# Moving the first Wk chunk to second place on its DMA ring and finishing the first four key tiles one after another

## The chip, the cores and the metric

The kernel runs on one core of a Trainium2 chip. The metric is the device time of one execution in microseconds; the figure for a kernel is the median of several executions. A separate execution is profiled; its trace gives the start and the duration of every instruction, the time at which every DMA landed, and the inferred releaser of every wait. All durations in the text come from that one execution.

## What is computed

Two branches are mixed by a gate. Branch A is a linear attention over `x` (2048 rows of 512) with 32 heads of 16; branch B is a token-mixing MLP over the layer-normed `x`. Cut to what matters:

```python
phi = lambda t: jnp.where(t > 0, t + 1, jnp.exp(t)) + 1e-6
q, k, v = split(x @ wqkv)                   # per head
pq, pk = phi(q), phi(k)
kv = einsum("bhsd,bhse->bhde", pk, v);  z = einsum("bhsd->bhd", pk)
o  = (pq @ kv) / (pq @ z)
a  = o @ wo
u  = gelu(einsum("bsd,sf->bdf", layernorm(x), w1) + b1)
b  = transpose(einsum("bdf,fs->bds", u, w2) + b2)
g  = sigmoid((x * gate_w).sum(-1))
out = g * a + (1 - g) * b
```

The value projection is not formed. Since `kv` is linear in `v = x Wv`, the kernel accumulates G, the product of `x` transposed with `pk`, over all rows and multiplies the small result by `Wv` afterwards.

## The kernel before, in words

The 2048 rows are 16 tiles of 128 (index t); the 512 features are four blocks of 128 (index k). The order of instructions is written out by hand: each engine carries out its own instructions in program order, and semaphores are placed between engines where data demand it. There are five stages:

1. **Start.** All loads are queued up. Eight of 128 KB come first, four on the ring of SyncE (SP) and four on that of ScalarE (ACT), issued by `load_x` (L124) and `load_wk` (L127): x tiles 0 to 3, then the four row blocks ("chunks") of Wk. Behind them SP issues the transposing loads of `xT` for tiles 4 and later (L130) and the rest of x. For the first four tiles `xT` is made on TensorE by `transpose_tile` (L193): four 128x128 transposes into a PSUM bank, then one copy out, on VectorE (L199) for tiles 0 and 2, on ScalarE (L197) for 1 and 3. Six matmuls on constants (`warm_up`, L108) run while the first load is under way, a seventh of 256 columns between the transposes of tiles 1 and 2.
2. **Keys.** `k_part(t, ks)` adds the named chunks to the key accumulator of tile t, one 128x512 matmul per chunk. `k_phi` turns the finished accumulator into `pk`: exp on ScalarE (L203), a min-add (L204) and a max-add (L207) on VectorE. For the first four tiles (`HEADS`) the chunks go outermost: chunk 0 for tiles 0 to 3, chunk 1 for tiles 0 to 3, chunk 2 likewise, and chunk 3 last; then the four `k_phi`. From tile 4 on a loop makes per tile four key matmuls, `k_phi`, the four G matmuls of tile t - 4 (`g_tile`), and on VectorE the layer-norm statistics of tile t - 3 (`ln_step`, L227 and L228). After the loop come `g_tile` of tiles 12 to 15.
3. **First part of the MLP with the queries.** Three accumulators of `u` and one query block per step.
4. **The rest of `u`,** with the small products of branch A between.
5. **Output.** Per row tile four matmuls of branch A and fourteen of branch B, then one combination on VectorE and a store.

All matmuls are recorded at L108, so the trace tells them apart by the accumulator: `wps` warm-up, `kacc` keys, `gacc` G, `qacc` queries, `uacc` MLP, `aps` and `yps` output; `pt` holds the transposes. Accumulators come from one pool of eight PSUM banks: one that is freed is given to the next that asks, and that one must wait until the former's last reader is done. G holds four of the eight through stage 2, so `kacc` of tile t takes the bank that tile t - 4 leaves.

Of the kernel before, what the change touches and what calls it, by code (L numbers as in the profile page):

```python
# [15 lines left out]
def kernel(  # L16
# [13 lines left out]
    nc = tc.nc  # L30
# [10 lines left out]
    ND = D // P  # L41
# [25 lines left out]
    def bank(name, dtype=FP32):  # L67
        return ps.tile([P, SC], dtype, name=name, tag="bank")
# [38 lines left out]
    def mm(o, lhsT, rhs, start, stop, **kw):  # L107
        nc.tensor.matmul(o, lhsT=lhsT, rhs=rhs, start=start, stop=stop, **kw)  # L108
# [14 lines left out]
    def load_x(q, t0, n):  # L123
        q.dma_start(out=xs[:, t0 : t0 + n, :], in_=x_view[:, t0 : t0 + n, :])  # L124

    def load_wk(q, k):
        q.dma_start(out=wk_sb[:, k, :], in_=wqkv_view[:, k, D : 2 * D])  # L127

    def load_xT(t0, n):
        nc.sync.dma_start(  # L130
            out=xT[:, :, t0 * P : (t0 + n) * P], in_=X[t0 * P : (t0 + n) * P, :], transpose=True
        )

    for i in range(2):
        load_x(nc.sync, 2 * i, 1)
        load_x(nc.scalar, 2 * i + 1, 1)
    for i in range(2):
        load_wk(nc.sync, 2 * i)
        load_wk(nc.scalar, 2 * i + 1)
    load_xT(4, 2)  # L140
    load_xT(6, 2)
    load_x(nc.sync, 4, 4)
# [39 lines left out]
    def warm_up(n, cols=SC):  # L182
        for _ in range(n):
            mm(wps[:, :cols], warm[:, 0:P], warm[:, :cols], True, True)
# [5 lines left out]
    def transpose_tile(t, on_act):  # L190
        pt = bank("pt", BF16)
        for k in range(ND):
            nc.tensor.transpose(pt[:, k * P : (k + 1) * P], xs[:, t, k * P : (k + 1) * P], ident[:])  # L193
        dst = xT[:, :, t * P : (t + 1) * P]
        src = pt[:].rearrange("p (k s) -> p k s", k=ND)
        if on_act:
            nc.scalar.activation(out=dst, in_=src, func=ACT.Copy)  # L197
        else:
            nc.vector.tensor_copy(out=dst, in_=src)  # L199
# [13 lines left out]
    def k_part(t, ks):  # L213
        if t not in kaccs:
            kaccs[t] = bank("kacc")
        for k in ks:
            mm(
                kaccs[t][:], xT[:, k, t * P : (t + 1) * P], wk_sb[:, k, :],
                k == 0, k == ND - 1,
            )  # L220

    def k_phi(t):
        phi(pk[:, t, :], kaccs.pop(t))

    def ln_stats(t):
        stats = work.tile([P, nc.vector.BN_STATS_DIM], FP32, name="stats", tag="stats", bufs=2)
        nc.vector.bn_stats(out=stats[:], in_=xs[:, t, :])  # L227
        nc.vector.bn_aggr(out=mv[:, t, :], in_=stats[:])  # L228

    def ln_rstd(g):  # L230
        s = slice(g * TPC, (g + 1) * TPC)
        nc.vector.tensor_scalar_add(out=veps[:, s], in0=mv[:, s, 1], scalar1=EPS)
        nc.gpsimd.tensor_tensor(out=rstd[:, s], in0=veps[:, s], in1=mhalf[:], op=ALU.pow)
# [36 lines left out]
    def ln_step(u):  # L270
        ln_stats(u)
        if u % TPC == TPC - 1:
            ln_rstd(u // TPC)

    HEADS = 4
    transpose_tile(0, False)
    transpose_tile(1, True)
    warm_up(1, 256)
    transpose_tile(2, False)
    transpose_tile(3, True)  # L280
    ln_step(0)
    ln_step(1)
    for k in range(ND - 1):
        for t in range(HEADS):
            k_part(t, (k,))
    for t in range(HEADS):
        k_part(t, (ND - 1,))
    for t in range(HEADS):
        k_phi(t)
    LAG = 4  # L290
    LN_LAG = 3
# [218 lines left out]
```

## Time and profile before

| what | value |
|---|---|
| median of 8 runs | 166.93 us (166.57 to 167.23) |
| the profiled execution | 166.53 us |
| its span, first to last instruction | 164.6 us |
| TensorE busy (PE) | 159.1 us, 97% of the span |
| VectorE busy (DVE) | 87.6 us, 53% |
| ScalarE busy (ACT) | 58.5 us, 36% |
| first key matmul starts | 5.56 us |

PE is TensorE's matmul side, PEld its weight loads, DVE VectorE, ACT ScalarE; a q after an engine's name is its sequencer, which issues DMAs. Times of instructions count from the start of the span. Matmuls overlap in their pipeline: a 128x512 matmul lasts 379 ns in the list of groups, but the next one starts 0.216 us after it, so the distance of starts is what a matmul costs.

### The profile page before, as it was taken

To read this page: it belongs to the slowest core of one execution; us is meant where nothing else is said; L and a number is where in the kernel's file an instruction comes from. 1 tells how busy PE (TensorE), PEld (TensorE's weight loads), DVE (VectorE), ACT (ScalarE), POOL (GpSimd) and SP (SyncE) were. 2 spreads that over 40 slices of the span, in tenths; PEclk is the share of its full clock that TensorE was granted. 3 is DMA by queue.
4 is the path that set the end of the run, shared out by engine and by line. 5 is a ranking of instruction groups with operands and counts; after the bars stand their busy time and mean duration, and the time that the engine had idled before them with its cause. 6 is when DMAs were issued, how large, how long until landed. Compare 5 with 4: busy or idle time off the path is not lost.

```text
span 164.6 us, 2059 instructions
## 1 busy us (share of the span) xinstructions
PE 159.1 (97%) x772; PEld 74.0 (45%) x786; DVE 87.6 (53%) x200; ACT 58.5 (36%) x90; POOL 18.3 (11%) x37
## 2 busy tenths in 40 slices
PE   7899999999999999999999999999999999999992
PEld 2534444444544444434444444444444444444471
DVE  0579999967999999109995301156221111111131
ACT  3364284848568374221332113111122221111110
POOL 5000702200110000001055500050000000000000
PEclk9999999999999999999999999999999999999999
DMA  5999999999900005800794499932010001101001
GB/s 147 243 249 235 295 354 334 349 347 349 303 25 0 0 0 154 292 4 0 258 307 115 158 298 310 327 120 88 32 36 32 32 32 46 49 33 36 32 32 32
DMA packets 29993, 25.05 MB, mean 152 GB/s; under 512 B 7776, under 2 KB 29408, under 8 KB 29984
## 3 DMA queue, kind: packets, MB, share of 16 engines
q1 hardware_dynamic: 27968, 22.02, 44.8%
q0 software_dynamic: 1440, 2.38, 5.1%
q10 hardware_dynamic: 576, 0.52, 1.0%
q8 instruction: 6, 0.10, 0.3%
q14 instruction: 3, 0.02, 0.0%
HBM read 21.11 MB, written 2.23 MB: 142 GB/s over the span
## 4 chain that ended last, share of the span: by engine, by line
PE 93%; DMA 2%; DVE 1%; issue 1%; SPq 0%; ACT 0%
PE yps L108 29%; PE uacc L108 29%; PE gacc L108 9%; PE qacc L108 8%; PE aps L108 8%; PE kacc L108 8%; DMA wk_sb<-in_A_wqkv_dram 2%; PE denps L108 1%; PE kvps L108 1%; PE wps L108 1%; SPq L124 0%; DVE pk L207 0%; ACT e L203 0%; DVE ot L473 0%; DVE e L204 0%
## 5 line engine op out<-in xcount | busy, mean ns | idle before, releaser
L108 PE MATMUL uacc<-hs,w1c 128*128 128x512 bf16 x218 | 51.6, 379 | 0.3
L108 PE MATMUL yps<-uT,w2c 128*128 128x512 bf16 (+1 forms) x235 | 50.8, 366 | 0.2
L473 DVE SCALAR_TENSOR_TENSOR ot<-yps,c,a_sc 128x512 bf16<-128x512 f32 (+1 forms) x17 | 12.2, 720 | 46.1 <-PE yps L108 46.1
L108 PEld LDWEIGHTS <-w2c 128*128 128x128 bf16 x238 | 23.3, 98 | 25.3
L108 PEld LDWEIGHTS <-w1c 128*128 128x128 bf16 x224 | 21.7, 98 | 26.0 <-issue 0.4
L458 ACT ACTIVATE a_sc<-aps,c,gg 128x512 f32<-128x512 f32 x16 | 12.5, 778 | 46.7 <-PE aps L108 43.0
L318 ACT ACTIVATE uT<-uacc,bcol 128x512 bf16<-128x512 f32 x14 | 9.3, 687 | 27.7 <-PE uacc L108 27.7
L108 PE MATMUL qacc<-xT,wq_sb 128*128 128x512 bf16 x64 | 16.4, 379 | 0.0
L108 PE MATMUL aps<-W2sb,pqT 128*128 128x512 bf16 x62 | 16.2, 379 | 0.1
L108 PE MATMUL kacc<-wk_sb,xT 128*128 128x512 bf16 x63 | 15.7, 379 | 0.5 <-DMA wk_sb<-in_A_wqkv_dram 0.4
L108 PE MATMUL gacc<-pk,xs 128*128 128x512 bf16 x62 | 15.7, 379 | 0.3 <-DVE pk L207 0.2
L243 ACT ACTIVATE hs<-xs,nmr,rstd 128x512 bf16<-128x512 bf16 x16 | 12.8, 804 | 3.1 <-DVE nmr L237 3.1
L203 ACT ACTIVATE e<-qacc 128x512 bf16<-128x512 f32 x16 | 9.6, 597 | 10.1 <-PE qacc L108 9.2
L203 ACT ACTIVATE e<-kacc 128x512 bf16<-128x512 f32 x16 | 9.0, 595 | 8.9 <-PE kacc L108 8.9
L414 POOL DMA_DIRECT2D rex<-rd_dram x16 | 9.5, 606 | 23.0 <-DVE pqT L416 18.1
L207 DVE SCALAR_TENSOR_TENSOR pk<-kacc,e 128x512 bf16<-128x512 f32 x16 | 11.1, 692 | 0.6
L207 DVE SCALAR_TENSOR_TENSOR pqT<-qacc,e 128x512 bf16<-128x512 f32 x16 | 11.1, 692 | 0.6
L204 DVE TENSOR_SCALAR e<-e 128x512 bf16<-128x512 bf16 x32 | 9.0, 282 | 4.3 <-ACT e L203 4.3
L227 DVE BATCH_NORM_STATS2 stats<-xs 128x6 f32<-128x512 bf16 x16 | 10.9, 682 | 0.0
L108 PEld LDWEIGHTS <-xs 128*128 128x128 bf16 x64 | 6.3, 98 | 8.1 <-issue 0.8
L401 DVE CUSTOM_DVE_ANT_0 junk<-xs,gw_b 128x512 bf16<-128x512 bf16 x16 | 9.8, 680 | 0.0
L108 PEld LDWEIGHTS <-xT 128*128 128x128 bf16 x64 | 6.2, 98 | 7.9 <-ACT xT L197 0.5
(64 smaller groups left out, 73.1 us busy)
## 6 DMA issues: line engine op xcount, KB each, us to landing
w2c<-in_B_w_dram SPq DMA_DIRECT2D x4, 1792.0 KB, 8.9
w1c<-in_B_w_dram SPq DMA_DIRECT2D x2, 2048.0 KB, 15.9
w1c<-in_B_w_dram SPq DMA_DIRECT2D x3, 1024.0 KB, 11.6
rex<-rd_dram POOLq DMA_DIRECT2D x16, 128.0 KB, 3.1
out_dram<-ot SPq DMA_DIRECT2D x15, 128.0 KB, 1.7
xs<-in_A_x_dram SPq DMA_DIRECT2D x3, 512.0 KB, 4.6
wq_sb<-in_A_wqkv_dram SPq DMA_DIRECT2D x1, 512.0 KB, 6.3
wv_sb<-in_A_wqkv_dram SPq DMA_DIRECT2D x1, 512.0 KB, 11.3
```

What stands on the lines that cost most here:

```text
L108: nc.tensor.matmul(o, lhsT=lhsT, rhs=rhs, start=start, stop=stop, **kw)
L203: nc.scalar.activation(out=e[:], in_=acc[:], func=ACT.Exp)
L204: nc.vector.tensor_scalar(out=e[:], in0=e[:], scalar1=1.0, scalar2=PHI_EPS, op0=ALU.min, op1=ALU.add)
L207: nc.vector.scalar_tensor_tensor(out=dst, in0=acc[:], scalar=0.0, in1=e[:], op0=ALU.max, op1=ALU.add)
L227: nc.vector.bn_stats(out=stats[:], in_=xs[:, t, :])
L243: nc.scalar.activation(out=hs[:, t, :], in_=xs[:, t, :], func=ACT.Identity, scale=rstd[:, t : t + 1], bias=nmr[:, t : t + 1],)
L318: nc.scalar.activation(out=uT[:, j, :], in_=acc[:], func=ACT.Gelu_apprx_tanh, bias=bcol[:, j : j + 1])
L401: nc.vector.tensor_tensor_reduce(out=junk[:], in0=xs[:, t, :], in1=gw_b[:], scale=1.0, scalar=0.0, op0=ALU.mult, op1=ALU.add, accum_out=gp ...
L414: nc.gpsimd.dma_start(out=rex[:], in_=src.unsqueeze(1).to_broadcast([8, HEAD, SC]))
L458: nc.scalar.activation(out=a_sc[:], in_=aps[:], func=ACT.Identity, scale=gg[:, t : t + 1], bias=c2[:, t : t + 1],)
L473: nc.vector.scalar_tensor_tensor(out=ot[:, :W], in0=yps[:, :W], scalar=c1[:, t : t + 1], in1=a_sc[:, cs], op0=ALU.mult, op1=ALU.add,)
```

## The change

The order of the eight first loads becomes x0, Wk0, x3, Wk2 on SP and x1, x2, Wk1, Wk3 on ACT (before: x0, x2, Wk0, Wk2 and x1, x3, Wk1, Wk3). The seventh warm-up matmul is left out. After the transposes of tiles 0 to 2 come the key matmuls of chunks 0 and 1 for these three tiles, then the transposes of tile 3. Then each tile in turn gets what it lacks (chunks 2 and 3; tile 3 all four) and its `k_phi` at once. The statistics of tile 1 are written after the transposes of tile 3; nothing else of VectorE's stands between.

```diff
-    for i in range(2):
-        load_x(nc.sync, 2 * i, 1)
-        load_x(nc.scalar, 2 * i + 1, 1)
-    for i in range(2):
-        load_wk(nc.sync, 2 * i)
-        load_wk(nc.scalar, 2 * i + 1)
+    load_x(nc.sync, 0, 1)
+    load_x(nc.scalar, 1, 1)
+    load_wk(nc.sync, 0)
+    load_x(nc.scalar, 2, 1)
+    load_x(nc.sync, 3, 1)
+    for k, q in ((1, nc.scalar), (2, nc.sync), (3, nc.scalar)):
+        load_wk(q, k)
...
     transpose_tile(1, True)
-    warm_up(1, 256)
     transpose_tile(2, False)
-    transpose_tile(3, True)
     ln_step(0)
+    for k in range(2):
+        for t in range(HEADS - 1):
+            k_part(t, (k,))
+    transpose_tile(HEADS - 1, True)
     ln_step(1)
-    for k in range(ND - 1):
-        for t in range(HEADS):
-            k_part(t, (k,))
     for t in range(HEADS):
-        k_part(t, (ND - 1,))
-    for t in range(HEADS):
+        k_part(t, range(2 if t < HEADS - 1 else 0, ND))
         k_phi(t)
```

## The prediction

> **What bounds the kernel now.** I read the page first (busy shares, chain that ended last), then TensorE's own waits, then the chain of waits and the timeline of the first 20 us, then the DMA view in narrow windows, last the end of the key stage.
>
> ```profile
> PE 159.1 (97%) x772; PEld 74.0 (45%) x786; DVE 87.6 (53%) x200; ACT 58.5 (36%) x90; POOL 18.3 (11%) x37
> PE 93%; DMA 2%; DVE 1%; issue 1%; SPq 0%; ACT 0%
> ```
>
> TensorE carries 93% of the chain, so anything that shortens or lengthens its stream shows up one to one. Its waits after the first instruction are these:
>
> ```profile
> PE kacc L108 <- DMA wk_sb<-in_A_wqkv_dram: 0.4, 1, 0.4
> PE gacc L108 <- DVE pk L207: 0.2, 1, 0.2
> ```
>
> Both lie in the stage that the change touches. The chain of waits there:
>
> ```profile
> 1.73 3.79 DMA wk_sb<-in_A_wqkv_dram
> 5.52 0.04 issue
> 5.56 2.98 PE kacc L108 x13
> 8.54 0.02 issue
> 8.56 0.61 ACT e L203
> 9.17 0.02 issue
> 9.19 0.31 DVE e L204
> 9.50 0.02 issue
> 9.52 0.70 DVE pk L207
> 10.22 0.04 issue
> 10.26 1.02 PE gacc L108 x4
> ```
>
> The path runs over the landing of chunk 0 (5.52), thirteen key matmuls until tile 0 is complete, its exp and two VectorE steps (2.07 us from the start of the thirteenth matmul, 8.15, to 10.21), then the first G matmul at 10.26. TensorE fills part of that time: the last of its 20 key matmuls (16 for tiles 0 to 3, 4 for tile 4) starts at 9.66. By the spacing of 0.216 us (0.86 us per four matmuls in the chain of the loop) the next could start at 9.87, and it starts at 10.26: **0.39 us lost**, of which the waits view sees 0.2 since it counts from modelled ends. Two smaller ones of this kind: tile 5's first key matmul starts 0.28 us after its forerunner (11.19), 0.05 us after VectorE has ended pk of tile 1 (11.14), whose PSUM bank it takes: **0.06 us**. And tile 15's first G matmul, in the timeline:
>
> ```profile
> 32.18 0.69 DVE L207 SCALAR_TENSOR_TENSOR pk<-kacc,e 128x512 bf16<-128x512 f32 x1
> 32.93 0.10 PEld L108 LDWEIGHTS <-xs 128*128 128x128 bf16 x1 [0.28 <-issue]
> ```
>
> It starts 0.05 us after pk of tile 15 ends (32.87), 0.38 us after the matmul before it (32.55): **0.16 us**. After that I find no stall above 0.2 us until the end of the span.
>
> **The loads.** Issue starts and times to landing from the DMA view in windows:
>
> ```profile
> xs<-in_A_x_dram SPq DMA_DIRECT2D x1, 128.0 KB, 2.9
> ...
> wk_sb<-in_A_wqkv_dram ACTq DMA_DIRECT2D x1, 128.0 KB, 4.0
> ...
> wk_sb<-in_A_wqkv_dram ACTq DMA_DIRECT2D x1, 128.0 KB, 4.5
> ```
>
> Together with the issue times (0.81, 1.25, 1.73, 2.2 on each ring) the four places of SP's ring land at 3.60, 4.19, 5.52, 6.25 and those of ACT's at 3.78, 4.38, 5.69, 6.72. All eight are of one size, so I keep a place's landing when what it carries is changed. A rule speaks against that: the Trainium skill's page "DMA: Bandwidth & Descriptors" (Queues, rings and completion order) says that completion isn't first-in, first-out per issuing engine. By the trace each ring's four landings are in order and 0.5 to 1.3 us apart, so I take the places. The bad end: Wk0 gains nothing from its place and lands at 5.52 still. Then the path worked out below begins with three matmuls at 5.56, 5.78 and 5.99 in place of 4.77 to 5.48, the next step starts at 6.21 in place of 5.73, and 0.48 us of the sum are lost (rival 2). The good end, a landing before 4.19, gives nothing more, since the copy of tile 0 ends at 4.72.
>
> **The change part by part.**
>
> *Loads.* Wk0 comes to 4.19 (from 5.52), x2 to 4.38 on ACT (from 4.19), x3 to 5.52 (from 4.38); Wk1, Wk2 and Wk3 keep 5.69, 6.25 and 6.72. Number and order of issue behind them stay. SP's first transposing load waits 1.2 us for an x load (waits of SP's queue; it starts 0.2 us after x0 lands, as the ninth DMA) and x0 is still first; the later ones meet x1 and Wk0, landed by then. So xT of tile 4 lands at 7.92 as before.
>
> *The seventh warm-up goes.* It holds 0.11 us (4.41 to 4.52), but tile 2's transposes need x2 at 4.38 anyway: they start near 4.42 and end near 4.81, VectorE's copy (0.42) near 5.27. Worth 0.1 us there, nothing at the end, since Wk1 comes later. "TensorE: Matmul & The Clock Gate" (Parts 1 and 4) warns that the array runs at half rate until about 3.4 us of activity, and that transposes don't count as activity. The row says that the switch is past: transposes are 0.107 us apart up to 4.26 and 0.056 from 4.36, before the removed matmul starts, and TensorE's idle gap that follows, 0.42 us, becomes shorter. By the rule read strictly it would cost as worked out under rival 3; by the row nothing. I take the row.
>
> *Chunks 0 and 1 of tiles 0 to 2.* Tile 0's copy ends at 4.72, tile 1's at 5.21, tile 2's near 5.27: the three chunk-0 matmuls start at 4.77, 5.26, 5.48. Chunk 1 lands at 5.69: 5.73, 5.95, 6.16. These six have all started by the time at which before only three had.
>
> *Tile 3's transposes* now wait in TensorE's stream for x3 (5.52) ahead of everything else; at 6.38 it is there. Four of 0.056 us: to 6.60. They only change places, so they cost nothing in sum. If x3 came later than 6.38, all that follows would shift one to one. ScalarE's copy runs 6.80 to 7.40 (it was 5.17 to 5.77), ahead of exp of tile 0.
>
> *Finish in turn.* Tile 0 chunk 2 starts at 6.60 (landed 6.25), chunk 3 at 6.82 (landed 6.72, ready 6.76). Nine matmuls remain from there, 1.94 us, so tile 4's first starts at 8.76; before it was 9.01. **Gain 0.25 us.** Tile 3's own start at 7.90, its copy done at 7.40; xT of tile 4 (7.92) is in time by 0.8 us.
>
> *pk of tile 0.* Complete at 7.20, exp from 7.36 (ScalarE's copy delays it by 0.12), pk done at 7.36 + 1.65 = 9.01. G of tile 0 can start at 8.76 + 4 x 0.216 = 9.62: no wait. **Gain 0.39.** pk of tile 1 follows by 0.93 (VectorE's distance in the timeline): 9.94, and tile 5 asks for that bank at 10.49: **gain 0.06.** The number of bank requests and the order of their release stay, so the bank is that of tile 1 still; this is inferred, not seen.
>
> *pk of tile 15.* VectorE is without an idle stretch from 9.19 to 32.87 in the timeline, so its start sets its end: 1.2 us earlier, 31.67. TensorE, 0.70 us earlier, asks at 32.07. **Gain 0.16.** ScalarE's exp stays 0.3 us or more ahead of VectorE.
>
> Sum: 0.25 + 0.39 + 0.06 + 0.16 = **0.86 us**. What is late next: nothing by 0.4 us; the landings after stage 2 lie far ahead of use (first W1 chunk 28.8 of some 33.6; xT of tile 12 at 17.4). The tail after the last matmul is unchanged. Profiled execution: 166.53 - 0.86 = 165.67, span 163.8. That execution is 0.40 under the median of the eight runs, and I take the same gain from the median: **166.05 us**.
>
> **Rivals.**
>
> 1. *Part of the gain.* Either Wk1 or Wk3 lands up to 0.4 us later than its place says, or tile 5 gets tile 2's bank (pk 10.86, so a start at 10.91 instead of 10.49). For: landings differ by 0.2 to 0.5 us between the two rings at one place. Against: bytes ahead are equal. Gain about 0.45: 166.5.
> 2. *It doesn't do what it says:* Wk0 lands no sooner than 5.52. Tile 3's transposes then stand in TensorE's stream after the first key matmuls instead of before, and tile 4 starts 0.22 us later than now; yet pk of tile 0 is still ready before G asks, so three stalls go: 0.86 - 0.48 = 0.38 gained, 166.55, close to what can be told from no change. For: landings are not bound to the order of issue (the rule above). Against: all eight landed in ring order.
> 3. *Slower: the clock gate.* With the warm-up gone and four transposes amid the key matmuls the array falls back to half rate for one window. Place: 4.4 to 8. Price: in 3.4 us matmuls 0.427 apart (as the six warm-up matmuls are) instead of 0.216, eight instead of sixteen, so 1.7 us lost; it decides from about four matmuls at half rate (4 x 0.21 = 0.86). For: the rule on transposes. Against: the rate had switched before, and idle time falls. Time: 166.93 + 1.7 - 0.86 = 167.8.
>
> **How the numbers follow.** Full gain 0.60 (own range 165.7 to 166.35), rival 1 0.20, rival 2 0.12, rival 3 0.08. A difference of 0.2% (0.33 us) is about what a measurement of this kernel can tell from no change. The full gain, most of rival 1 (0.17) and half of rival 2 (0.06) are faster by more: 0.83; the rest of the two is the same: 0.09; rival 3 is slower: 0.08. The range 165.6 to 166.75 holds the first three but for their edges.
>
> **What would show it.** Right: Wk0 lands near 4.2 to 4.5; the first key matmul starts near 4.8, tile 0's chunk 3 at 6.8, tile 4 at 8.8, G of tile 0 near 9.6 without a wait on pk, G of tile 15 without one. Wrong: a TensorE wait on x3 before the transposes of tile 3, key matmuls 0.427 apart after 4.4, tile 5 waiting for pk of tile 2, Wk1 landing beyond 6 or Wk3 beyond 7.

## The result and the profile after

| what | before | after |
|---|---|---|
| median | 166.98 us (31 runs, 166.57 to 167.37) | 166.24 us (11 runs, 165.71 to 166.76) |
| ratio of times | | 0.9957, 95% interval 0.9946 to 0.9968 |
| profiled execution | 166.53 us, span 164.6 | 166.31 us, span 164.2 |
| tile 0's chunk 3 starts | 8.15 | 7.23 |
| tile 4's first key matmul | 9.01 | 9.18 |
| first G matmul (tile 0) | 10.26 | 10.04 |
| G of tile 15 starts | 32.93 | 32.49 |

The change makes the kernel 0.74 us faster by the medians; 0.86 was forecast. The two traces differ by only 0.45 us in span, and that difference needs an explanation too. In all ratios, runs more than 1.5% above the fastest of their kernel are left out.

TensorE's own waits in the changed kernel:

```profile
PE wps L108 <- PEq L493: 0.8, 1, 0.8
PE kacc L108 <- DMA wk_sb<-in_A_wqkv_dram: 0.2, 1, 0.2
```

The wait of G on `pk` has gone from the list. What is left after the program's first instruction is a wait for Wk, and the chain of waits says for which chunk:

```profile
1.74 4.37 DMA wk_sb<-in_A_wqkv_dram
6.11 0.04 issue
6.15 0.81 PE kacc L108 x3
6.96 0.22 PE pt L194 x4
7.18 3.02 PE kacc L108 x14
10.20 0.86 PE gacc L108 x4
```

From 6.15 until it is in G the chain holds nothing but TensorE: three matmuls of chunk 1, tile 3's four transposes, then the rest of the keys and straight into G (a chain piece begins where its forerunner's record ends, so the 10.20 here is a matmul that starts at 10.04). VectorE and ScalarE, which stood in the chain before between 8.56 and 10.22, are out of it. The landing that starts it is chunk 1 (issued at 1.74, landed at 6.11), not chunk 0 as before. Of the loads' places, second place on SP and third on ACT in the DMA view by windows:

```profile
wk_sb<-in_A_wqkv_dram SPq DMA_DIRECT2D x1, 128.0 KB, 2.9
...
wk_sb<-in_A_wqkv_dram ACTq DMA_DIRECT2D x1, 128.0 KB, 4.4
```

Wk0 is in at 4.16 (forecast 4.19); Wk1, with 4.4 in place of 4.0, at 6.11 (forecast 5.69). At the end of the key stage, in the timeline:

```profile
31.19 2.11 PE L108 MATMUL gacc<-pk,xs 128*128 128x512 bf16 x9
31.33 0.69 DVE L208 SCALAR_TENSOR_TENSOR pk<-kacc,e 128x512 bf16<-128x512 f32 x1
```

pk of tile 15 ends at 32.02, while TensorE is in an unbroken run of G matmuls that reaches tile 15 at 32.49: no wait, where before there was one of 0.16.

### The profile page after: what moved, and what is told of

Same layout as the page of the kernel before. It is cut to its first block, busy times and chain, and to the rows that moved or that the text cites. A ratio compares the mean times of both kernels' runs of the same rounds, so it can differ in the third digit from the quotient of the medians.

```text
span 164.2 us, 2057 instructions
## 1 busy us (share of the span) xinstructions
PE 159.1 (97%) x771; PEld 74.0 (45%) x785; DVE 87.8 (53%) x200; ACT 58.7 (36%) x90; POOL 18.2 (11%) x37
## 4 chain that ended last, share of the span: by engine, by line
PE 94%; DMA 3%; issue 1%; ACTq 1%; DVE 0%
PE uacc L108 29%; PE yps L108 29%; PE qacc L108 8%; PE gacc L108 8%; PE aps L108 8%; PE kacc L108 8%; DMA wk_sb<-in_A_wqkv_dram 3%; PE denps L108 1%; PE kvps L108 1%; ACTq L124 1%; PE wps L108 1%; DVE ot L472 0%; PE pt L194 0%; PE zps L108 0%; PE pt L323 0%
## 5 line engine op out<-in xcount | busy, mean ns | idle before, releaser
L108 PE MATMUL kacc<-wk_sb,xT 128*128 128x512 bf16 x63 | 16.2, 385 | 0.2 <-DMA wk_sb<-in_A_wqkv_dram 0.2
L269 DVE TENSOR_TENSOR zacc<-zacc,pk 128x512 f32<-128x512 f32 x14 | 9.6, 685 | 0.2
```

The lines of the kernel that those rows point to most:

```text
L269: nc.vector.tensor_tensor(out=zacc[:], in0=first, in1=pk[:, t, :], op=ALU.add)
```

## A sum that holds in every trace

Each run below left a trace of one execution of its own. Two things matter in it: when tile 4's first key matmul starts, and how much TensorE loses afterwards to waits on `pk` (distance of starts less 0.216). The span is the sum of the two and a constant of 155.02 us; that holds within 0.02 in all fourteen traces, of which these are eight:

| kernel (trace) | tile 4 starts | waits on pk | sum + 155.02 | span |
|---|---|---|---|---|
| before | 9.01 | 0.61 | 164.64 | 164.65 |
| before, second trace | 9.70 | 0.62 | 165.34 | 165.34 |
| after | 9.18 | 0 | 164.20 | 164.20 |
| after, second trace | 9.38 | 0 | 164.40 | 164.41 |
| only the loads | 9.79 | 0.62 | 165.43 | 165.43 |
| only TensorE's order | 11.35 | 0 | 166.37 | 166.37 |
| warm-up kept | 8.98 | 0 | 164.00 | 164.02 |
| only tile 3 last | 9.55 | 0 | 164.57 | 164.59 |

So everything that the change does, it does before tile 4 or at these three waits. Theory A was that the waits (0.61) carry the gain and that Wk1's landing sets the start; theory B, that the gain comes from the earlier start on Wk0; theory C, that the missing warm-up explains the shortfall.

## The experiments

Ratios are to the kernel before, timed beside each run, with 95% intervals; they can differ by 0.1% from the quotient of two medians.

**Second traces of both kernels (no edit).**

> The kernel before once more, for a second trace. Its profiled execution (166.53) lies at the low end of its runs (166.6 to 167.4), while that of the changed kernel (166.31) does not; so the two traces differ by 0.4 us in span where the medians differ by 0.7 to 0.9. If the trace shown was a favourable one: this trace has a span of 164.8 to 165.3, the same three waits on pk (0.39, 0.06, 0.16), and its key matmuls begin 0.2 to 0.5 us later than 5.56 or at half rate. If the medians differ for another reason: a span near 164.6 again and the difference sits outside of the span. Ratio 1.000 within 0.002.

> The changed kernel itself once more, for a second trace and a tighter time. Theory A (three waits on pk at the G matmuls and at tile 5's bank have gone, 0.61 us in sum, and the start of tile 4 is set by the landing of Wk1 in the third place of ACT's ring): ratio to before 0.995 to 0.997, no wait of G on pk in the trace, Wk1 landing anywhere from 5.6 to 6.2 and the first matmul of tile 4 at Wk1's landing plus 3.07. Theory B (the gain comes from the earlier start on Wk0): the gain goes with the landing of Wk0, near 4.2, and not with Wk1.

Measured: before 167.16 us, ratio 0.9999 (0.9989 to 1.0008); after 166.19 us, ratio 0.9933 (0.9911 to 0.9955). The chain of waits of the second trace of before:

```profile
1.73 4.22 DMA wk_sb<-in_A_wqkv_dram
...
5.99 3.24 PE kacc L108 x13
...
10.21 0.70 DVE pk L207
10.91 0.04 issue
10.95 1.02 PE gacc L108 x4
```

The chain has the form of the first trace, 0.4 to 0.7 us later. Wk0 landed at 5.95 here and at 5.52 in the first trace (0.43 of the 0.69 us by which tile 4 is later), and the first key matmuls come 0.38 and 0.31 apart before the spacing falls to 0.216 (the other 0.26). The waits are the same to 0.01. So the trace that the prediction was built on was a favourable one: span 164.6, where the 27 runs of before timed beside this one have spans of 164.8 to 165.3, with a median of 165.1. In the second trace of after Wk1 lands at 6.31, a little beyond the expected 5.6 to 6.2, and tile 4 starts at Wk1's landing plus 3.07, as expected, with Wk0 at 4.11 as early as in the first. The ratio is better than the 0.995 to 0.997 expected.

**The two halves of the change apart.** Only the new order of loads (`load_x` and `load_wk` as after, TensorE as before); only the new order on TensorE, the seventh warm-up matmul left out (loads as before):

> The new order of the eight loads with the old order on TensorE, the seventh warm-up matmul included. Theory A: slower than before by about 0.5 us (ratio 1.003), since the transposes of tile 3 wait for x3 in the third place (5.56) before any key matmul may start, so tile 0's chunk 3 starts near 8.6 (8.15 before) and pk and the three waits move with it. Theory B: faster than before by 0.3 to 0.7 us, since Wk0 is there at 4.2.

> The new order on TensorE with the old order of the loads (Wk0 third on SP's ring). Theory A: the three waits go here too; key matmuls from 5.56, chunk 1 from 6.2, tile 4 near 9.23 (9.01 before), so 0.4 us faster than before in the trace (ratio 0.9975), as rival 2 of the prediction had it. Theory B: no gain, ratio 1.000 or above.

Only the loads: 167.64 us, ratio 1.0045 (1.0023 to 1.0068), slower. TensorE's waits in its trace:

```profile
PE pt L194 <- DMA xs<-in_A_x_dram: 0.2, 1, 0.2
PE gacc L108 <- DVE pk L208: 0.2, 1, 0.2
```

Wk0 was in at 4.50 and helped nothing: tile 3's transposes stand before the first key matmul and wait for x3 (5.54), and the wait on `pk` is there in full. Five of its 22 runs lie apart, at 169.1 to 169.5; the other 17 have a median of 167.55, 0.44 us above before's 167.11, so it is slower without them too. Theory B falls. Only the order: 167.54 us, ratio 1.0016 (0.9979 to 1.0054), in two groups, which neither theory expected, seven runs at 166.5 to 167.1 and seven at 168.0 to 168.9. Its profiled execution is of the upper group:

```profile
5.70 2.72 PE L108 MATMUL kacc<-wk_sb,xT 128*128 128x512 bf16 x6 [0.78 <-DMA wk_sb<-in_A_wqkv_dram]
8.22 0.63 PE L193 MATMUL pt<-ident,xs 128*128 128x128 bf16 x4
8.64 1.57 PE L108 MATMUL kacc<-wk_sb,xT 128*128 128x512 bf16 x4
```

Six matmuls take 2.72 us, as the six warm-up matmuls did; their starts, 0.427 apart, fall to 0.216 only at about 9.8. That is rival 3's half rate, and the distance of the groups' medians, 168.50 and 166.76, agrees with its price of 1.7 us. But it isn't a fall back, as rival 3 had it: the transposes before 5.70 are 0.107 apart too, so the full rate had never come. The granted clock (PEclk) doesn't show it: 1.00 in a stretch at half rate, with 12 matmuls and transposes, and in one at full rate, with 18:

```profile
core 0: us, PE busy (x) PEld busy (x) DVE busy (x) ACT busy (x) POOL busy (x), PEclk, DMA share, GB/s
5.70:9.20 3.50, 3.50 (x12) 1.57 (x12) 1.23 (x4) 0.31 (x1) 0.00 (x0) 1.00 1.02 208
9.90:13.40 3.50, 3.50 (x18) 1.60 (x17) 2.93 (x7) 2.63 (x5) 0.00 (x0) 1.00 1.02 215
```

The lower group's middle, 166.76, lies 0.35 us below before's median of 167.11, near the 0.4 expected; of that group there is no trace.

**The warm-up matmul.** Put back into the changed kernel; put back into the order-only kernel; taken out of the kernel before:

```diff
     transpose_tile(1, True)
+    warm_up(1, 256)
     transpose_tile(2, False)
```

> The changed kernel with the seventh warm-up matmul put back between the transposes of tiles 1 and 2. Theory A: no difference from the changed kernel beyond 0.1 us (ratio to before 0.995 to 0.997), since what follows waits for Wk1 anyway; the array may reach full rate earlier than 5.2, where it did in the changed kernel's trace, without moving the first chunk-1 matmul. Theory C (the missing warm-up keeps the array at half rate longer and that is the shortfall against the forecast): faster than the changed kernel by 0.2 to 0.4 us.

> TensorE's new order with the old loads, as in the order-only kernel, but with the seventh warm-up matmul put back. If the two groups of times of the order-only kernel (166.5 to 167.1 and 168.0 to 168.9) come from the clock gate, which then sees neither the warm-up nor an early key matmul: one group only, near 166.6 (ratio 0.997 to 0.998), key matmuls 0.216 apart from 6.5 on at the latest. If the warm-up has nothing to do with it: two groups again.

> The kernel before with nothing changed but the seventh warm-up matmul left out: the price of that edit when Wk0 comes third. If the clock gate misses its switch when there is no early key matmul: two groups of times as in the two kernels with the old loads and the new order, the one near 167.0, the other 1.5 to 1.9 us above it with key matmuls 0.427 apart until about 8.5, and more of them in the slow group than the two in 57 of the kernel before; median 167 to 168.8. If the edit costs nothing here: one group, ratio 0.999 to 1.001.

Put back into the changed kernel: 166.20 us, 0.9949 (0.9937 to 0.9960), like the changed kernel without it; theory C falls. Order-only with it: eight runs at 166.35 to 166.98, two at 168.5 and 168.9, ratio 0.9982 (0.9957 to 1.0007); one group was expected, so that expectation was wrong. Taken out of before: 167.12 us, 0.9996 (0.9987 to 1.0005), one group; two groups were thought possible and didn't come. The edit thus costs nothing in either kernel, and the two groups don't hang on it alone. They were seen in order-only (7 of 14, and 2 of 10 with the warm-up), in loads-only (5 of 22) and twice in 57 runs of before; never in the 28 of the changed kernel, 17 of which were timed together with those of order-only and loads-only. In these three kernels the first key matmul comes late, at 5.6 to 6.0, but so it does in the next kernel, at 5.70, which has one group; that one was timed on another chip, where before had one group too. What makes the difference between before and the order-only kernel was not settled. Idle time before the first key matmul is a candidate: 0.78 and 0.85 us in the two order-only traces, 0.42 to 0.58 in those of before and of before without the warm-up, 0.08 in the next kernel; but in loads-only the array idles only 0.25, ahead of tile 3's transposes.

**Which part of the order carries it.** The kernel before with old loads, warm-up and transposes, only tile 3's key matmuls last; and the changed kernel with the finish in turn undone:

```diff
-    for k in range(ND - 1):
-        for t in range(HEADS):
-            k_part(t, (k,))
-    for t in range(HEADS):
-        k_part(t, (ND - 1,))
-    for t in range(HEADS):
-        k_phi(t)
+    for k in range(2):
+        for t in range(HEADS - 1):
+            k_part(t, (k,))
+    for t in range(HEADS):
+        k_part(t, range(2 if t < HEADS - 1 else 0, ND))
+        k_phi(t)
```

> The kernel before with old loads, the seventh warm-up and all four tiles' transposes in their old places; only the key matmuls are reordered: chunks 0 and 1 for tiles 0 to 2, then each tile in turn, tile 3 last with all four chunks. So tile 0's chunk 3 is the eighth of the sixteen instead of the thirteenth, and the sixteen begin and end as before. If the three waits on pk are 0.61 us of the gain and hang on this order alone: no such wait, tile 4 starting 3.5 to 3.7 us after the first key matmul, ratio to before 0.996 to 0.997, and what the changed kernel has beyond that (0.1 to 0.4 us) belongs to the loads. If chunk 2 or 3 of Wk comes later than tile 0 now asks for it (1.3 and 1.5 us after the first key matmul; 0.7 and 0.9 to 1.2 after Wk0 by the traces): up to 0.1 us of it is lost. Two groups of times as in the order-only kernel would mean that the clock gate is disturbed by the order itself and not by the idle time that tile 3's later transposes leave.

```diff
-    for t in range(HEADS):
-        k_part(t, range(2 if t < HEADS - 1 else 0, ND))
-        k_phi(t)
+    for k in range(2, ND):
+        for t in range(HEADS - 1):
+            k_part(t, (k,))
+    k_part(HEADS - 1, range(ND))
+    for t in range(HEADS):
+        k_phi(t)
```

> The changed kernel with the finish in turn undone: after the transposes of tile 3 chunk 2 for tiles 0 to 2, chunk 3 for tiles 0 to 2, then tile 3, and the four phi after that. Tile 0's chunk 3 then starts two matmuls (0.43 us) later, at 7.6 to 7.9. Theory A (VectorE, busy without a break, carries its start over to pk of tile 15): G of tile 0 still doesn't wait (pk near 9.8, asked at 10.0 to 10.2), but pk of tile 15 comes 0.4 later and G of tile 15 waits for it by about 0.2; 0.1 to 0.3 us slower than the changed kernel, ratio to before 0.996 to 0.998. If finishing in turn does nothing: ratio as the changed kernel's, 0.994 to 0.996, and no wait at tile 15.

Only tile 3 last: 166.35 us, ratio 0.9965 (0.9953 to 0.9977), all 18 runs in one group, 165.99 to 166.86. In its chain of waits twenty key matmuls pass into G with nothing between:

```profile
5.70 4.88 PE kacc L108 x20
10.58 0.86 PE gacc L108 x4
```

The loads are those of before and the start is no better, yet 0.35% are gained: the waits alone are 0.61 us, 0.37% of 166.98. Tile 4 starts 3.85 us after the first key matmul, not 3.5 to 3.7, since that trace runs at half rate until about 6.6. Chunks 2 and 3 were in time (6.37 and 6.84, asked for at 7.40 and 7.61). The finish in turn undone: 166.13 us, 0.9943 (0.9928 to 0.9958), no slower than the changed kernel. The expectation of a wait at tile 15 was wrong by little: pk of tile 15 ends at 32.24 and its G matmul, due at 32.33, isn't held up. The expectation had that matmul one place too early, since one record is missing in the changed kernel's trace. So turn by turn or chunk by chunk doesn't matter; that tile 3's four matmuls come after tile 0's last does. Three of them stood ahead of it before: 0.65 us of work, more than the longest wait of 0.39.

**A faster version?** Wk1 and x3 exchanged between the rings; tile 3's transposes ahead of chunk 1; the same with the warm-up:

> The changed kernel with Wk1 and x3 exchanged between the rings (Wk1 third on SP, x3 third on ACT). If the shortfall against the forecast is a matter of the ring (SP's third place before ACT's, 5.56 against 6.11 in the first trace of the changed kernel): chunk 1 starts near 5.75, tile 4 near 8.8, 0.2 to 0.4 us faster than the changed kernel (ratio to before 0.992 to 0.994). If the third places of both rings are simply uncertain between 5.5 and 6.3: no difference beyond 0.15 us.

> The changed kernel with the transposes of tile 3 moved ahead of the chunk-1 matmuls, into the time in which TensorE waits for Wk1 (0.24 to 0.50 us idle in the traces of the changed kernel). If x3 lands before Wk1, as in both of these traces (5.56 against 6.11, 6.13 against 6.31), up to 0.2 us faster than the changed kernel, tile 4 starting at Wk1's landing plus 2.85 instead of 3.07. If x3 comes later than Wk1 (6.01 against 5.81 in the kernel with the warm-up kept), up to 0.2 slower: in sum 0.0 to 0.2 faster, ratio to before 0.993 to 0.996.

> The changed kernel with the transposes of tile 3 ahead of chunk 1 and with the seventh warm-up matmul put back, the candidate for a version faster than both. The trace of the one without the warm-up has key matmuls at half rate (0.427 apart) from 4.73 to 6.0, so that TensorE was never idle and chunk 1 began at 6.33, 0.2 after Wk1. If the warm-up brings the full rate by 4.4: chunk 1 begins 0.05 us after Wk1 (5.7 to 6.1), tile 4 near 8.7 to 8.9, 0.1 to 0.3 us faster than the changed kernel, ratio to before 0.992 to 0.994. If the rate's switch is left to chance anyway: 0.994 to 0.996.

Exchanged: 166.38 us, 0.9952 (0.9937 to 0.9967). Wk1, third on SP, landed at 6.10, so the ring isn't the reason for the late landing. In that trace the half rate lasts until about 6.8, into the matmuls of chunk 1, and tile 4 starts at 9.64, 0.47 later than Wk1's landing plus 3.07: the changed order too can lose time to it. Transposes first: 166.09 us, 0.9943 (0.9929 to 0.9957); with the warm-up 166.22 us, 0.9946 (0.9932 to 0.9960). In the trace of the one without:

```profile
4.73 1.49 PE L108 MATMUL kacc<-wk_sb,xT 128*128 128x512 bf16 x3
6.01 0.49 PE L194 MATMUL pt<-ident,xs 128*128 128x128 bf16 x4
6.33 1.03 PE L108 MATMUL kacc<-wk_sb,xT 128*128 128x512 bf16 x4
```

The transposes fill the idle time, but the three matmuls before them run at half rate (0.427 apart) and take up what was saved. In the trace with the warm-up the full rate is there by about 3.5, before that matmul runs (3.87), and tile 4 starts at 8.90, within the 8.7 to 8.9 expected; the times are no better for it. None of the three can be told from the changed kernel.

## Why the prediction was right, and where it was off

- *The three waits on pk, 0.39 + 0.06 + 0.16:* right to 0.01. Both traces of before have them, neither of the changed kernel's has, and by the kernel with only tile 3 last they account for 0.6 of the 0.74 us. Tile 5 waits for no bank in them.
- *The start of tile 4, 0.25 earlier:* this term was mis-sized. Its step "I keep a place's landing when what it carries is changed" held for Wk0 (4.16), x2 (4.35) and x3 (5.56) and failed for Wk1 by 0.42 (6.11), which sets the path. Tile 4 came at 9.18, not 8.76, 0.17 later than in the trace of before. In all 14 traces the third place lands anywhere from 5.52 to 6.13 on SP (median 5.84) and from 5.69 to 6.31 on ACT (median 5.94). The numbers that I took for constants, 5.52 and 5.69, are the lowest of each.
- *Why the medians still agree nearly:* the kernel before also starts later in usual executions, as its start hangs on Wk0 in a third place and, in the second trace, on two matmuls at half rate; the sum has neither. The medians of the runs' spans, 165.1 before and 164.2 after, give 0.9 us (of the session with the second trace of after), the two traces shown 0.45; the medians of the times say 0.74 to 0.92. By the sum of the traces these spans put tile 4 at 9.46 before and 9.18 after (an estimate): 0.28 gained where 0.25 was forecast, but both some 0.4 later than the prediction's 9.01 and 8.76. That the two errors, the favourable trace of before and Wk1's landing, are of one size is luck.
- *Tile 3's wait for x3:* none, as forecast (x3 at 5.56, asked for at 6.80). *Wk0's earlier landing:* right in size, but by itself worth nothing (loads only: slower). It lets three matmuls pass before Wk1; for the whole of the loads' part 0.1 to 0.2 us remains (166.35 against 166.24 and 166.19), within the intervals. *SP's first transposing load* was misread, without harm: in every trace it starts about 0.02 us after x1 lands (3.80 and 3.78 in before), so it waits for x1, the first on ACT in both kernels, and not for x0.
- *The warm-up:* no cost, by the two kernels with that edit alone. The argument for it, that the switch to full rate is past when the removed matmul starts, was not sound: in the second trace of before the half rate lasts until about 6.6, and in the changed kernel the switch came between 5.2 and 5.5 instead of 4.3, hidden behind the wait for Wk1.
- *Rival 1* describes the trace (Wk1 late by 0.4, 0.45 us of span gained); of the medians the first, 0.74, lies between it and the full gain, the second, 0.92, above both. *Rival 2* didn't come: Wk0 landed early each time. *Rival 3* didn't come in the changed kernel, but half rate and its price are real in the order-only kernel, as a switch that comes late and not as a fall back: without the new loads the same order on TensorE loses 1.7 us in half of its runs. That is the case for keeping the loads with this order.

## What to carry to other kernels

When an engine waits for the result of a chain through two others, look for work of its own that may be done after the chain's first step instead of before it: moving tile 3's four matmuls behind tile 0's last closed three waits at once, one of them more than 20 us later, at no cost. A landing time read from one trace is a sample: before a sum rests on it, compare the traced execution with the spread of the runs. And an early order of work may put off the switch to full rate: one order on TensorE cost 1.7 us in half of its runs with the old loads, and in none of 28 with the new.

## What was not expected of the hardware

TensorE's half rate leaves no mark in the granted clock: 1.00 in a stretch with matmuls 0.427 us apart and in one with 0.216. It is read from the distance of starts alone. In the order-only kernel it lasted until about 9.8 us although matmuls, with four transposes among them, had been running without a break since 5.70, some four microseconds; in the trace of the same order with the warm-up until 10.3, in all others it ended between 3.5 and 6.8. The Trainium skill's "TensorE: Matmul & The Clock Gate" (Part 1) says that full rate comes after about 3.4 us of sustained activity, counted in windows that run freely. An estimate from the page's 3.4 us fits one window missed: 9.8 and 10.3 are 3.4 us after 6.4 and 6.9, near the 6.2 to 6.8 at which five other traces switch, and 3.4 us at half rate cost 1.7 us, the distance of the groups. That is a reading and not shown; why some edits of this study bring forth two groups of times and others don't, no run here explains. Eight equal loads on two rings landed in ring order in all 14 traces, but the third of a ring anywhere within 0.6 us.
